# One written sequence of all steps in place of a list scheduler, in a fused attention and Fourier-mixing kernel

## The chip, the cores and the metric

The kernel runs on one core of a Trainium2 chip. A core has a matrix engine (TensorE, PE here), three engines for elementwise work (VectorE, DVE; ScalarE, ACT; GpSimd, POOL), and a queue engine (SyncE, SP) that issues transfers; POOL issues transfers too. Each engine runs its own list of instructions strictly in order, and lists wait for one another through semaphores. The metric is the time of one execution in device microseconds; the median of 3 runs before is 578.95 us (578.54 to 579.04).

## The reference

Inputs are q, k, v (8 batches, 12 heads, 448 tokens, 64 per head) and two weight matrices, 768 x 3072 and 3072 x 768; all float32.

```python
q_n = q / (norm(q) + 1e-6);  k_n = k / (norm(k) + 1e-6)
attn = softmax(q_n @ k_n.T / tau)              # tau = 0.1
x = (attn @ v) as (8, 448, 768)
u = x + real(fft over 448 tokens and 768 channels)(x)
un = (u - mean(u)) / sqrt(var(u) + 1e-6)
out = u + relu(un @ w_ch1) @ w_ch2
```

## The kernel before, in words

Everything of a batch b carries the suffix _b in the names of its steps. A batch goes through three stages.

**Attention.** The loads (ld_q, ld_k, ld_t for the tails on SP, ld_v on POOL) bring in q, k, v. The norms are squares on ACT (sq, L759 and L883), sums on DVE (ss, L762 and L885), then ln, nrm on ACT (L698, L700), eps and rcp on DVE (L701, L702), and the scaling by them (sc, L781 and L785 on DVE or POOL in batches 0 and 1, L896 on POOL later). In batches 0 and 1 the scaled rows are transposed by matmuls (tk, tq, tt, L808 to L833) and copied out of PSUM (ek, eq, et, L799 and L843); from batch 2 on a transposing transfer on SP does it (tr, L902). Then, for each of six pairs of heads j, come the scores (qk j, L973, and L986 for the tail tokens), the exponentials on ACT (ex j, L951), the product with v (pv j, L1004 and L1010), and its division by the sums on DVE (rd j, x j, L1028 and L1030).

**Fourier transform.** Sums and differences of halves on DVE (fa, f0, f1, g, e, L1047 to L1094) shorten it, then there are two groups of matmuls with cosine and sine tables (fs, L1134 and L1138; fd, L1181, L1188, L1191), with a copy between (te, L1159), and the sums that give u (qe on ACT, pq and u on DVE, L1222, L1233, L1245). Each tile of 128 tokens is normalised (ba, L1270; bs, L1275; ln2, rs, L1278 and L1280; un, L1282) and transposed into UNT, in batch 0 by matmuls (tn, L1292, copied out by eu, L1300), later by a transfer on SP (tru, L1303).

**Feed-forward.** h (L1350) multiplies by w_ch1, with a relu on ACT or DVE (L1366) after every 512 columns of PSUM; y and m (L1494) multiply by w_ch2. In the m products two tiles of tokens are done with seven products of half size in place of eight, for which DVE adds up pieces of the hidden values (s1 to s4, L1593); in the last two batches the first multiplication is done so too (p, L1445, with its sums c and k). A result is put together on ACT, POOL and DVE (fa, fm, fv, L1514 and L1519; fin, L1530) and stored (st on SP, sc_ on POOL, L1552).

**What sets the order.** Each step is added to a plan with its engine (or a choice of engines), its duration, a priority, and the steps that it depends on. `schedule` then makes the order of every engine at once: it goes through a modelled time, and at each point picks, among the steps that are ready, the one with the best priority; steps that can run on ACT or DVE go to the one that takes them first. The table SHIFT adds a number to the priority of 338 steps. `emit` writes each engine's list in that order. Before it, `fill` puts filler matmuls (L1737) into PE's list where the plan has PE idle for at least 0.36 us. PSUM is handed out in the plan too: two slots "M" for the feed-forward and three double slots "G" for the rest; a step that needs a slot waits for the last user of the one it gets.

In the plan, a qk that directly follows an h, y, m or p step is charged 0.095 us more (MODE), and a step of DVE that falls into one of certain POOL steps is moved behind its piece (PORT, PIECE).

Of the kernel before, what the change touches and what calls it, by code (L numbers as in the profile page):

```python
# [79 lines left out]
SHIFT = {  # L80
    "iotad": {0: 76.7149}, "tpd": {1: 15.2941}, "ktd0": {0: 169.0303}, "ix3": {0: -59.6164}, "ix4": {0: 735.3976}, "vz1": {0: 116.8365},
    "pads": {0: 761.6515}, "sins": {0: 15.0098}, "ldt0": {0: 217.8585}, "ldt1": {0: -95.8889}, "sind": {0: -207.551}, "sinp": {0: 240.8715},
# [59 lines left out]
}  # L142

# [58 lines left out]
class Plan:  # L202
# [54 lines left out]
    def schedule(self):  # L257
# [46 lines left out]
        for op in self.ops:  # L304
            if cnt[op] == 0:
                put(op)
# [1491 lines left out]
```

## Time and profile before

| | |
|---|---|
| Runs | 578.95 us median (578.54 to 579.04) |
| Span of the profiled execution, first to last instruction | 575.2 us; the page gives no total for this execution, and the median run is 3.75 us above the span |
| Busy: PE, DVE, ACT, POOL | 555.8, 430.6, 385.3, 220.3 us |
| Filler matmuls | 156 |
| First matmul, end of the last | 7.46 us, 571.7 us |
| First h0_0 (start of the feed-forward of batch 0) | 48.46 us |
| Transfers | 62.20 MB, mean 108 GB/s, highest in the first 100 us |

A line of the groups gives the code line, the engine, the operation, output<-input and count, then busy time and the mean of one, then the idle time ahead of it and what ended it. In a line of the timeline the first number is the start in us, the second the time from the first start to the last end of the merged instructions; a wait stands in brackets at the end. A wait is put down to the releaser that came last by the profile.

### The profile page before, as it was taken

Reading aid. Unit: us, or ns where it says so; the run is one execution under the profiler, and the core shown is the slowest. Engines: PE = TensorE matmul, PEld = TensorE weight load, DVE = VectorE, ACT = ScalarE, POOL = GpSimd, SP = SyncE. Lnnn points to the kernel's source line nnn. Section 1 sums busy time; section 2 is a strip of 40 time slices with the busy share of each in tenths; the row PEclk is TensorE's granted clock in tenths of the full one; section 3 lists DMA queues with packets and bytes.
Section 4 is the critical chain, followed back from the end, with each engine's and each line's share of the span. In section 5 each row is a group of like instructions: output and inputs, shape, how many; then the busy total and the mean of one; then the engine's idle time right before and its main releaser. Section 6 shows DMA issues by size and latency. Waiting matters only on the chain.

```text
span 575.2 us, 16313 instructions
## 1 busy us (share of the span) xinstructions
PE 555.8 (97%) x6766; PEld 436.2 (76%) x6766; DVE 430.6 (75%) x917; ACT 385.3 (67%) x724; POOL 220.3 (38%) x332
## 2 busy tenths in 40 slices
PE   3899999999999999999999999999999999989997
PEld 3569787676787686878788787778778787959694
DVE  8989968996669869975669669776778579986262
ACT  7898885564876885687558875577637853747270
POOL 7534414356329544612370724523270210041303
PEclk9999999999999999999999999999999999999999
DMA  9999999975459739952595429743591210023001
GB/s 188 224 233 171 166 186 130 171 152 111 111 94 103 178 76 135 142 127 62 112 121 93 102 80 147 150 84 85 89 113 29 43 57 28 2 43 72 28 28 56
DMA packets 187898, 62.20 MB, mean 108 GB/s; under 512 B 166800, under 2 KB 185616, under 8 KB 187824
## 3 DMA queue, kind: packets, MB, share of 16 engines
q1 hardware_dynamic: 129856, 38.35, 33.7%
q0 software_dynamic: 57968, 22.81, 30.9%
q8 instruction: 53, 0.87, 0.6%
q14 instruction: 21, 0.17, 0.1%
HBM read 51.90 MB, written 11.01 MB: 109 GB/s over the span
## 4 chain that ended last, share of the span: by engine, by line
PE 60%; DVE 4%; ACT 2%; issue 0%; DVEq 0%; ACTq 0%
PE PS L1494 23%; PE PS L1350 20%; PE PS L1445 6%; PE PS L1010 4%; PE PS L973 3%; DVE U L1233 1%; PE PS L1004 1%; PE PS L986 1%; ACT E L951 1%; DVE ACG L1222 1%; ACT F L1275 1%; PE PS L1134 1%; PE PS L1191 1%; DVE SM L885 1%; DVE HQ L1593 1%
## 5 line engine op out<-in xcount | busy, mean ns | idle before, releaser
L1350 PE MATMUL PS<-UNT,W1b 128*128 128x256 bf16 (+1 forms) x1872 | 186.1, 256 | 1.2 <-DMA UNT<-F 0.6
L1350 PEld LDWEIGHTS PS<-UNT,W1b 128*128 128x128 bf16 x1872 | 155.5, 98 | 20.1 <-issue 2.7
L951 ACT ACTIVATE E<-PS 128x900 bf16<-128x900 f32 (+1 forms) x192 | 148.0, 827 | 19.1 <-PE PS L973 16.6
L1494 PE MATMUL PS<-W2b,HQ 128*128 128x384 bf16 x768 | 133.1, 326 | 0.0
L896 POOL TENSOR_TENSOR QH<-STG,SM 128x256 bf16<-128x256 f32 x126 | 82.3, 679 | 91.9 <-DVE SM L702 73.3
L1494 PEld LDWEIGHTS PS<-W2b,HQ 128*128 128x128 bf16 x768 | 73.3, 98 | 46.2 <-issue 0.7
L1519 POOL TENSOR_TENSOR OUTB<-OUTB,U 128x192 f32<-128x192 f32 x66 | 43.2, 675 | 138.5 <-ACT OUTB L1514 137.3
L1366 ACT ACTIVATE HQ<-PS 128x512 bf16<-128x512 f32 x81 | 48.2, 595 | 40.0 <-PE PS L1350 39.5
L1494 PE MATMUL PS<-TX,HQ 128*128 128x384 bf16 (+2 forms) x408 | 69.7, 321 | 1.8 <-ACT MV L1278 1.6
L883 ACT ACTIVATE QH<-STG 128x384 f32<-128x384 f32 x84 | 42.7, 520 | 25.8 <-DVE SM L885 21.3
L1494 PEld LDWEIGHTS PS<-TX,HQ 128*128 128x128 bf16 x408 | 38.4, 98 | 25.7 <-ACT MV L1278 2.0
L1593 DVE TENSOR_TENSOR HQ<-HQ 128x1536 bf16<-128x1536 bf16 (+1 forms) x69 | 49.5, 721 | 9.9 <-ACT HQ L1366 7.1
L885 DVE TENSOR_REDUCE SM<-QH 128x6 f32<-128x384 f32 x84 | 44.7, 544 | 11.3 <-ACT QH L883 11.0
L1010 PE MATMUL PS<-VB,E 128*128 128x65 bf16 x1152 | 51.4, 193 | 0.0
L1366 DVE TENSOR_SCALAR HQ<-PS 128x512 bf16<-128x512 f32 x45 | 31.0, 688 | 23.8 <-PE PS L1350 23.4
L1010 PEld LDWEIGHTS PS<-VB,E 128*128 128x128 bf16 x1152 | 47.7, 97 | 1.2
L1552 POOL DMA_INDIRECT out_dram<-OUTB,IDX x21 | 23.8, 1134 | 56.9 <-DVE OUTB L1530 51.7
L1004 PE MATMUL PS<-VZ,E 128*128 128x130 bf16 x192 | 41.6, 219 | 0.5 <-ACT E L951 0.2
L973 PE MATMUL PS<-QK 64*128 64x225 bf16 (+2 forms) x864 | 39.6, 227 | 0.1
L1233 DVE SCALAR_TENSOR_TENSOR U<-ACG,X 128x768 bf16<-128x768 f32 (+4 forms) x39 | 39.1, 1015 | 0.8
L1530 DVE TENSOR_TENSOR OUTB<-PS,OUTB 128x384 f32<-128x384 f32 x33 | 18.2, 553 | 25.7 <-PE PS L1494 21.9
L1514 ACT ACTIVATE OUTB<-PS 128x384 f32<-128x384 f32 x33 | 16.1, 488 | 29.5 <-PE PS L1494 29.1
(191 smaller groups left out, 793.6 us busy)
## 6 DMA issues: line engine op xcount, KB each, us to landing
STG<-in_q_dram SPq DMA_DIRECT2D x18, 384.0 KB, 4.0
STG<-in_k_dram SPq DMA_DIRECT2D x18, 384.0 KB, 3.8
VB<-in_v_dram POOLq DMA_DIRECT2D x24, 192.0 KB, 7.1
W1b<-in_moe_w_ch_dram POOLq DMA_DIRECT2D x12, 384.0 KB, 7.7
W2b<-in_moe_w_ch_dram POOLq DMA_DIRECT2D x12, 384.0 KB, 7.2
out_dram<-OUTB SPq DMA_DIRECT2D x7, 384.0 KB, 3.4
W2b<-in_q_dram SPq DMA_DIRECT2D x2, 576.0 KB, 10.0
W2b<-in_k_dram SPq DMA_DIRECT2D x2, 576.0 KB, 10.7
```

The lines of the kernel that those rows point to most:

```text
L885: P.add("dve", lambda v, o=SS[:, i, H // ns * x:H // ns * (x + 1)], sq=sq: v.tensor_reduce(o, sq.rearrange("p (h d) -> p h d", d=DH), AX.X ...
L896: r = v.tensor_tensor(v3(qh)[:, h:h + 4], v3(buf)[:, h:h + 4], RN[:, i, h:h + 4].unsqueeze(2).to_broadcast((128, 4, DH)), AluOp.mult)
L951: return a.activation(o, self.PS[:, bk:bk + nc_, 0:SQ2], ACTF.Exp, scale=1.0 / self.tau)
L973: i = pe.matmul(self.PS[:, bk + h, c0:c0 + n], self.KT[r, jj, kt * 128:(kt + 1) * 128], self.QT[r, jj, cols], start=True, stop=True)
L1004: r = pe.matmul(o, st(6), self.VZ[:, j, :], start=not split, stop=(split and i == 0), skip_group_check=True)
L1010: r = pe.matmul(o[:, 65 * h:65 * h + 65], st(2 * kt + h), self.VB[:, kt, 2 * j + h, :], start=(split and i == h == kt == 0), stop=((not sp ...
L1233: self.snu.append(P.add("dve", lambda v: v.scalar_tensor_tensor(two(U[o0:o0 + n, ut, :]), src, 1.0, two(X[i0:i0 + n, x, :]), AluOp.mult, A ...
L1350: r = pe.matmul(self.PS[:, bk, x * n:(x + 1) * n], self.W1b[:, j, ft * 128:(ft + 1) * 128], self.UNT[:, j, cs], start=(j == 0), stop=(j == ...
L1366: return e.activation(o, i, ACTF.Relu) if e is self.nc.scalar else e.tensor_relu(o, i)
L1494: r = pe.matmul(self.PS[:, bk, 0:n], lhs(f), rhs(f), start=(start and f == 0), stop=(stop and f == NF // 2 - 1), skip_group_check=True)
L1519: r = g.tensor_tensor(self.OUTB[:, ob, xs], self.OUTB[:, ob, xs], self.U[:, ut, xs], AluOp.add)
L1593: P.add("dve", lambda v: v.tensor_tensor(cs(o), cs(a), cs(bq), op), 0.16 + 0.3 * len(ks), -0.5, f"{nm}{ks[0]}_{b}", reads=rd, writes=[x fo ...
```

## The change

The table SHIFT and the choice by priorities go. In their place stands SEQ, a list of all 2850 steps in the order in which the plan takes them. An entry is 5 x (number of the step) + (number of the engine: 0 PE, 1 ACT, 2 DVE, 3 POOL, 4 SP), so it fixes both the order on each engine and the engine of each step that has a choice. `schedule` goes through the list and works out times as before (they still decide PSUM slots and where filler goes); it no longer decides on an order. The steps, their dependences and their instructions are the same, but for one: the step finz_7 near the end also counts as a writer of OUT1.

```diff
-SHIFT = {
-    "iotad": {0: 76.7149}, "tpd": {1: 15.2941}, "ktd0": {0: 169.0303}, "ix3": {0: -59.6164}, "ix4": {0: 735.3976}, "vz1": {0: 116.8365},
...
-}
+SEQ = [
...
+    7569, 9719, 8443, 8473, 8453, 8449, 8459, 9799, 9774, 7685, 7690, 7682, 7697, 7216, 7206, 7700, 7970, 7976, 8000, 7705, 7711, 7715, 7720, 7730, 7735,
...
+]
@@ schedule
-        while left:
-            best = None
-            for e in self.ENGS:
-                cands = []
-                for op in ready[e]:
-                    rt = rtime(op, e)
...
-                tmin = min(c[0] for c in cands)
-                t, op = min((c for c in cands if c[0] <= tmin + 1e-9), key=lambda c: (c[1].prio, c[1].seq))
...
-            t, e, op = best
-            for e2 in op.engs:
-                ready[e2].remove(op)
+        for code in SEQ:
+            op, e = self.ops[code // 5], self.ENGS[code % 5]
+            assert all(d.start is not None for d in op.deps.union(op.order))
+            t = max(rtime(op, e), free[e])
+            if op.acquire is not None:
+                t = max(t, slot_time(op)[0] + op.margin)
+            if e == "sp" and sync[-2]:
+                t = max(t, sync[-2].end - DMA_LAT)
             op.eng = e
...
-                                f"finz_{b}", reads=self.unames(b, u1), writes=["OUT1z"], after=(m7,), tiles=(b1,))
+                                f"finz_{b}", reads=self.unames(b, u1), writes=["OUT1z", "OUT1"], after=(m7,), tiles=(b1,))
...
-            op.prio = round(op.prio + SHIFT.get(op.name, {}).get(k, 0), 4)
         self.est = self.P.schedule()
```

Decoded and set beside the order before, engine by engine (steps; steps that leave their former order, as the least number that would have to be moved):

| | PE | ACT | DVE | POOL | SP |
|---|---|---|---|---|---|
| steps before | 969 | 693 | 859 | 195 | 134 |
| steps after | 969 | 672 | 880 | 195 | 134 |
| out of order | 168 | 280 | 370 | 72 | 43 |

109 steps change their engine: 60 from ACT to DVE, 39 from DVE to ACT, 5 from DVE to POOL, 5 from POOL to DVE. The places that the prediction speaks of, before and after (a step that stands several times has several parts):

```text
SP, first loads       before  q1 k0 q0 t0 q2 t1 k1 t2 k2
                      after   q1 t0 t1 k0 q0 k1 q2 t2 k2
POOL, batch 0         before  ld_v2 ld_v0 ld_v1 ld_v3 ktd0 scQ0 ... W1_0
                      after   ld_v2 ktd0 ix6 ld_v1 ld_v3 ix0 scK0 ld_v0 W1_0
ACT, batch 0          before  ex2 ex2 ex2 ex2 et2 et2 ex3 ex3 ex3 ex3
                      after   ex2 ex2 ex2 ex2 ex3 ex3 et2 ex3 ex3           (the other et2 on DVE)
DVE, batch 0          before  u0 u0 u0 ba0 un0 u1 u1 eu00 u1 u1
                      after   u0 u0 ba0 un0 ssT0_1 eu01 cd0 u1 u0          (eu00 on ACT, behind bs0)
PE, second h0_0       before  h19 h20 tn1 tn2 tq0_1 h21 h22 h23 tt0_1 tk0_1 tq2_1 tk2_1 qk00_1 tk1_1 tq1_1 h0 h1
                      after   h19 tq1_1 tt0_1 tq2_1 tq0_1 tn1 tn2 h20 tk0_1 h21 h22 h23 tk1_1 qk00_1 h0 tk2_1 h1
DVE, batch 1          before  pq1 pq1 ba0 u1 u224 fin11_0 u1 ss4_2 ba1 un0 u1 ss4_2 ba3 ba2 fin20_0 un1
                      after   pq1 pq1 u1 u224 ss3_2 u1 ba1 fin11_0 un0 ss3_2 ba2 ktd2 un1
PE, batch 1           before  m20_1 m60_1          after   m20_1 qk00_2 m60_1
DVE, batch 2          before  un0 fin31_1 u1 un1   after   un0 fin31_1 un1 fin21_1 u1
DVE, batch 6          before  pq1_7 pq1_7 s11 c31 u1_7 s12 u224_7 s30 ba0_7 s20
                      after   c31 c31 s10 c2r1 c3r1 s12 s11 ba3_7 s30 s20 pq1_7 pq1_7
PE, batch 4           before  h10_2 h11_2 h20_2 ... h23_2 y02_2 (3) y12_2 (3) y22_2 (2) qk00_4 y22_2
                      after   h10_2 qk00_4 h11_2 h20_2 ... h23_2 qk0t_4 y02_2 (3) qk10_4 y12_2
POOL, batch 4         before  fv0p_2 sc6_4 sc0_5 sc5_4   after   fv0p_2 sc6_4 sc5_4
SP, batch 4           before  tr6_4 ld_k0_5 ld_q1_5 ld_q0_5 tr5_4   after   tr6_4 tr5_4 ld_k0_5
```

More of the change, by code (lines that the diff above doesn't have):

```diff
@@ L78 @@
 }
-SHIFT = {
-    "iotad": {0: 76.7149}, "tpd": {1: 15.2941}, "ktd0": {0: 169.0303}, "ix3": {0: -59.6164}, "ix4": {0: 735.3976}, "vz1": {0: 116.8365},
-    "pads": {0: 761.6515}, "sins": {0: 15.0098}, "ldt0": {0: 217.8585}, "ldt1": {0: -95.8889}, "sind": {0: -207.551}, "sinp": {0: 240.8715},
[59 rows of a table removed]
-}
+SEQ = [
[117 rows of a table added]
+]
 LATE = {r"W[12]_\d+": 1.5, "tmd": 2.0, r"sq\d_\d": 1.5, r"sq[KQT]\d_1": 1.5, r"ktd\d": 2.0, r"qdup\d": 2.0, r"qk\d._[2-7]": 1.5, r"pv\d\d_[2-7]": 1.5, r"pv\d\d_1": 1.0, r"h\d+_[1-7]": 0.5}
@@ L257, in schedule @@
     def schedule(self):
-        nxt = {}
-        cnt = {}
-        for op in self.ops:
-            cnt[op] = len(op.deps.union(op.order))
-            for d in op.deps.union(op.order):
-                nxt.setdefault(d, []).append(op)
-        ready = {e: [] for e in self.ENGS}
         port = []
@@ L298, in drain @@
             return qs
-        def put(op):
-            for e in op.engs:
-                ready[e].append(op)
-        for op in self.ops:
-            if cnt[op] == 0:
-                put(op)
-        left = len(self.ops)
         slots = {n: [None] * k for n, k in self.pools.items()}
@@ L322, in slot_time @@
             return free_at[-1][0], [i for _, i in free_at]
-        while left:
-            best = None
-            for e in self.ENGS:
-                cands = []
-                for op in ready[e]:
-                    rt = rtime(op, e)
-                    if op.acquire is not None:
-                        st = slot_time(op)
-                        if st is None:
-                            continue
-                        rt = max(rt, st[0] + op.margin)
-                    if e == "sp":
-                        rt = max(rt, sync[-2].end - DMA_LAT if sync[-2] else 0.0)
-                    cands.append((max(rt, free[e]), op))
-                if not cands:
-                    continue
-                tmin = min(c[0] for c in cands)
-                t, op = min((c for c in cands if c[0] <= tmin + 1e-9), key=lambda c: (c[1].prio, c[1].seq))
-                if e in ("act", "dve"):
-                    wait = tmin + 0.7 * op.times[e][1]
-                    t2, op2 = min((c for c in cands if c[0] <= wait), key=lambda c: (c[1].prio, c[0]))
-                    if op2.prio >= 9 and (op.prio > op2.prio + 60 or op2.prio < 40 and op.prio > op2.prio + 0.5 and t2 < tmin + 0.25):
-                        t, op = t2, op2
-                if best is None or (t, e) < best[:2]:
-                    best = (t, e, op)
-            t, e, op = best
-            for e2 in op.engs:
-                ready[e2].remove(op)
+        for code in SEQ:
[6 more added lines that the diff above has]
+                t = max(t, sync[-2].end - DMA_LAT)
             op.eng = e
@@ L390, in schedule @@
             self.order[e].append(op)
-            left -= 1
-            for n in nxt.get(op, ()):
-                cnt[n] -= 1
-                if cnt[n] == 0:
-                    put(n)
         return max(op.end for op in self.ops)
@@ L1725, in build @@
             self.ffn(b)
-        seen = {}
-        for op in self.P.ops:
-            k = seen[op.name] = seen.get(op.name, -1) + 1
-            op.prio = round(op.prio + SHIFT.get(op.name, {}).get(k, 0), 4)
         self.est = self.P.schedule()
```

175 rows, old and new, of tables (SEQ, SHIFT) are left out of this document.

## The prediction

> **What bounds the kernel now.** I read the page first, then the time by stretches, then who made TensorE (PE) wait, then the chain of waits and single places of the timeline. From the page, the span and PE's row:
>
> ```profile
> span 575.2 us, 16313 instructions
> PE 555.8 (97%) x6766; PEld 436.2 (76%) x6766; DVE 430.6 (75%) x917; ACT 385.3 (67%) x724; POOL 220.3 (38%) x332
> ```
>
> The same by stretches (length, busy time of PE, PEld, DVE, ACT, POOL, then PE's granted clock):
>
> ```profile
> 0.00:48.40 48.40, 35.94 (x518) 27.82 (x518) 43.20 (x103) 41.44 (x67) 27.32 (x58) 1.00 1.31 211
> 48.40:78.40 30.00, 29.27 (x414) 25.01 (x413) 26.11 (x63) 26.07 (x52) 11.77 (x17) 1.00 1.30 166
> 78.40:118.00 39.60, 38.98 (x379) 27.77 (x380) 31.79 (x75) 25.90 (x56) 14.35 (x22) 1.00 0.98 158
> 118.00:190.00 72.00, 71.88 (x733) 55.14 (x732) 55.47 (x107) 47.83 (x90) 39.05 (x50) 1.00 0.73 118
> 190.00:260.00 70.00, 69.76 (x835) 53.97 (x833) 55.14 (x123) 52.84 (x109) 31.55 (x45) 1.00 0.73 129
> 260.00:504.00 244.00, 243.92 (x3149) 195.19 (x3148) 181.16 (x380) 159.03 (x292) 77.55 (x114) 1.00 0.49 82
> 504.00:506.30 2.30, 0.68 (x5) 0.20 (x3) 1.88 (x4) 1.38 (x4) 1.17 (x1) 1.00 0.02 4
> 506.30:571.70 65.40, 65.38 (x744) 51.12 (x744) 35.54 (x69) 30.78 (x59) 17.23 (x30) 1.00 0.19 44
> 571.70:575.20 3.50, 0.00 (x1) 0.00 (x0) 0.29 (x1) 0.00 (x0) 0.36 (x1) 0.89 0.31 112
> ```
>
> Part of PE's time at the start is filler (line 1737, matmuls that only keep PE at work):
>
> ```profile
> 0.00:48.40 48.40, 12.66 (x150) 9.88 (x150) 1.00 1.31 211
> 48.40:78.40 30.00, 0.59 (x8) 0.35 (x6) 1.00 1.30 166
> ```
>
> And PE's waits from 78.4 on (line, releaser: us, times, longest):
>
> ```profile
> PE PS L1494 <- ACT MV L1278: 1.6, 1, 1.6
> PE PS L1350 <- DMA UNT<-F: 0.6, 1, 0.6
> PE PS L986 <- ACT E L951: 0.2, 1, 0.2
> ```
>
> The reader is to see two regimes. Up to 48.4 us (the first h0_0, the first step of the feed-forward part) PE has 48.4 - 35.9 = 12.5 us of nothing and 12.7 us of filler: there the chain through ScalarE (ACT, 41.4 of 48.4 busy) and VectorE (DVE, 43.2 busy) sets the time. From there to 571.7 PE is full: it stands 0.73 + 0.62 + 0.12 + 0.24 + 0.08 + 1.62 + 0.02 = 3.4 us in 523, and 0.6 more is filler. An order can't shorten the matmuls (the granted clock is 1.00 as long as PE works), so the change can win only at the start and in these 4 us; it can lose anywhere, because each engine works strictly in its list's order, and one late step holds all behind it.
>
> **The change part by part.** It neither adds nor removes a step: 2850 before and after. I decoded the list (number = 5 x step + engine) and set both orders side by side. 109 steps change engine, 60 from ACT to DVE and 39 back, so DVE gets 21 more; out of their former order are 168 of 969 on PE, and many on the others. Since PE has so little slack, I price the places where it stood, in time order.
>
> (a) The start. ACT's idle time in the exponentials of batch 0:
>
> ```profile
> 25.68 0.55 ACT L951 ACTIVATE E<-PS 128x450 bf16<-128x450 f32 x1 [0.27 <-PE PS L986]
> 27.05 0.67 ACT L843 ACTIVATE KTD<-PS 64x192 bf16<-64x192 f32 x2 [0.81 <-PE PS L833]
> 27.99 0.92 ACT L951 ACTIVATE E<-PS 128x900 bf16<-128x900 f32 x1 [0.27 <-PE PS L973]
> ```
>
> The new order puts one copy of 0.67 / 2 = 0.33 us (et2_0) on DVE and the other behind two ex3_0 steps, so up to 0.33 + 0.27 + 0.81 + 0.27 = 1.7 us of ACT's time can go. A second place is the way to h0_0:
>
> ```profile
> 45.84 0.55 DVE L1245 SCALAR_TENSOR_TENSOR U<-PS,X 128x384 bf16<-128x384 f32 x1
> 47.85 0.55 DVE L1300 CAST UNT<-PS 128x384 bf16<-128x384 f32 x1
> 48.46 0.73 PE L1350 MATMUL PS<-UNT,W1b 128*128 128x128 bf16 x10
> ```
>
> Before, a third u0_0 (0.55) stands ahead of ba0_0 and un0_0, and two u1_0 (0.55 each) ahead of the cast eu00_0 that frees h0_0. The new order moves all three behind: 0.5 at the first, and 0.3 to 0.5 at the second, where bs0_0 on ACT is now the last thing ahead of a copy. All of it together is 1.7 + 1.0 = 2.7. Against it stands the new order of the first loads (rival B). I take -1.5, a little over half, because DVE's row of this stretch leaves little room for what it receives; bounds -2.7 and +0.5 (a copy more on a full DVE, 0.55).
>
> (b) 48.4 to 78.4 us: 0.73 idle and 0.59 filler. Before, tn1_0, tn2_0 and seven transposes of batch 1 stand between h20_0 and the second h0_0, five of them behind the last h23_0; now they are spread from h19_0 to the second h1_0, with products between. I take -1.0; bounds 0 and -1.3.
>
> (c) 117 us: PE waits 0.6 for the transposed tile UNT. Between pq1_1 and un1_1 DVE's list loses two ss4_2, a u1_1 and fin20_0 and gains two ss3_2 and a ktd2: the tile leaves earlier. -0.6; bounds 0 and -0.6.
>
> (d) 118 to 260 us: 0.36 idle. qk00_2 now stands ahead of the product m60_1 that waited for s20_1, and un1_2 ahead of a u1_2. -0.3; bounds 0 and -0.4.
>
> (e) 504 us, the largest. PE waits, by the releaser's name for ACT, but in the code for s20_6, the DVE step that writes what m61_6 reads:
>
> ```profile
> 499.96 1.02 DVE L1222 TENSOR_TENSOR ACG<-PS,ACG 128x388 f32<-128x388 f32 x2
> 501.70 0.95 DVE L1233 SCALAR_TENSOR_TENSOR U<-ACG,X 97x768 bf16<-97x768 f32 x1
> 503.40 1.76 POOL L1519 TENSOR_TENSOR OUTB<-OUTB,U 128x192 f32<-128x192 f32 x2 [35.16 <-ACT OUTB L1514]
> 503.48 1.28 DVE L1593 TENSOR_TENSOR HQ<-HQ 128x1536 bf16<-128x1536 bf16 x1
> 505.22 0.96 DVE L1593 TENSOR_TENSOR HQ<-HQ 128x1536 bf16<-128x1536 bf16 x1 [0.39 <-DVE MV L1270]
> 506.32 0.97 PE L1494 MATMUL PS<-TX,HQ 128*128 128x384 bf16 x5 [1.64 <-ACT MV L1278]
> ```
>
> s20_6 ends at 505.22 + 0.96 = 506.18 and PE goes on 0.14 later. Ahead of s30_6 and s20_6 stood two pq1_7 (1.02), u1_7 (0.95) and u224_7; now all of them stand behind. u224_7 pays for two short relus that DVE receives there, the rest is 1.97 us of DVE, more than PE's 1.64. What then comes later is un1_7 and its transpose; another u1_7 that stood ahead of un1_7 goes behind it too, which pays for most. -1.5; bounds 0 and -1.6.
>
> The row shows s20_6 starting at 505.22, just after POOL's two pieces end (503.40 + 1.76 = 505.16), though DVE was idle 0.39. The Trainium skill, SBUF — State Buffer, section "SBUF: two separate sides", says that DVE and GpSimd share one pair of ports as an exclusive lock, and that the loser blocks for the whole instruction. The trace agrees, and it speaks against this place: should s20_6 come just behind the start of POOL's step again, it would wait one piece, 1.76 / 2 = 0.9, and (e) would bring 0.7 in place of 1.5, the sum 0.8 less.
>
> (f) Entering a qk step (its matmuls use 64 rows):
>
> ```profile
> 264.58 1.31 PE PS L1350 x12
> 311.26 1.42 PE PS L1350 x12
> 82.16 0.34 PE L1010 MATMUL PS<-VB,E 128*128 128x65 bf16 x6
> 82.34 1.03 PE L1350 MATMUL PS<-UNT,W1b 128*128 128x256 bf16 x8
> 216.85 0.35 PE L1010 MATMUL PS<-VB,E 128*128 128x65 bf16 x6
> 217.12 0.37 PE L973 MATMUL PS<-QK 64*128 64x225 bf16 x4
> ```
>
> Next to a qk, twelve matmuls take 1.42, elsewhere 1.31. The plan charges this only where a qk follows a product directly: 50 times before, 43 now, 7 x 0.11 = 0.8 to win. But behind a pv step the qk costs the same: from the last six matmuls of a pv to the next step 0.18 to a product, 0.27 to a qk. Counted behind anything but a qk, entries are 95 before and 96 now. So 0; bounds -0.8 and +0.1.
>
> (g) The step finz_7 also writes OUT1 now, so it waits for the store of the tile before. That store lies a whole tile of products earlier; 0. The tail of 3.5 us stays.
>
> (h) New waits of PE, which no row of before can show. Lower bound 0; upper bound: all that (a) to (e) remove, 4.9, since the order of before shows that an order can hold that much. Nearer to the long stretch 260 to 504, where the old order left 0.08 us in 244: +1.0.
>
> Sum: -1.5 - 1.0 - 0.6 - 0.3 - 1.5 + 0 + 1.0 = -3.9, so a span of 571.3. The page gives no total time for its execution; the median of the runs shown, 578.95, lies 3.75 above its span. Kept, that makes 575.0.
>
> **The rivals.** A, the forecast: 575.0.
>
> B, the start brings nothing, as its loads set it. On SP's queue the first k and q loads of batch 0 now stand behind both pairs of tail loads, and on POOL the load ld_v0_0 behind scK0_0. For it: the DMA share of that stretch is 1.31, the highest of all. Against it: the bytes are the same, and the larger k1 load is now ahead of q2, which ACT takes later. Without (a): 575.0 + 1.5 = 576.5.
>
> C, no change: the waits move to other places and (h) reaches its upper bound: 575.0 + 3.9 = 578.9. For it: 109 changes of engine and a plan that gains only by its own durations. Against it: the places (c), (d), (e) are freed by more than their waits.
>
> D, slower: the attention of batch 4 is drawn too far ahead. Before:
>
> ```profile
> 242.32 2.82 SPq L902 DMA_TRANSPOSE QK<-QH  x1
> 250.15 0.78 PE L973 MATMUL PS<-QK 64*128 64x128 bf16 x24
> QK<-QH SPq DMA_TRANSPOSE x42, 3.1
> 312.68 0.65 PE PS L1494 x4
> ```
>
> The last transpose of its k and q (tr5_4) is issued until 245.14 and lands some 3.1 later, at 248.2, 2.0 ahead of qk00_4. In the new order qk00_4 stands ahead of five h steps and eight y02_2 to y22_2 steps, 13 x 0.65 = 8.5 us of PE work earlier, so it is due at 241.7. If it can only start at s, PE has 8.5 us more left than before had at 250.15; the end moves by 8.5 - (250.15 - s), and of the gains only (e) lies behind it, 1.5: together s - 243.15. For s above that it is slower; at 245.7, half way to 248.2, by 2.55: 581.5. Queued behind it on PE are all these h and y steps; ACT's ex0_4 wait with it. For it: SP held tr5_4 for 2.82 us and it landed last of its batch. Against it: sc5_4, which made tr5_4 late, now goes ahead of batch 5's sc0_5 on POOL, and tr5_4 ahead of three loads of batch 5 on SP.
>
> **How the numbers follow.** A 0.50, B 0.17, C 0.14, D 0.15, and 0.04 for nearly all the upper bounds at once (-2.7 - 1.3 - 0.6 - 0.4 - 1.6 = -6.6, 572.3, or 571.6 with (f)). What a measurement can tell from no change is 0.2%, 1.2 us. Faster: A, B nearly whole and the last, 0.70; within: mostly C, 0.13; slower: D and the tail of C, 0.17. The range goes from 571.8, near all bounds at once, to 580.0, short of D's middle; A's own is 572.5 to 577.
>
> **What would show it.** First h0_0 (line 1350's first matmul) near 47 in place of 48.46; the filler at line 1737 down; the waits of 0.6 at 117 and 1.64 at 504 gone; PE's idle time from there to its end near 1.5. B shows as h0_0 still at 48; D as a wait of line 973 for a transpose between 238 and 248; C as new rows in PE's waits. The forecast is wrong if PE's idle time after h0_0 stays at 3.4 or more, or if h0_0 comes later.

## The result: slower, and where the time stands in the profile after

The changed kernel takes 602.9 us (601.2 to 603.8) where the kernel before takes 579.0 (578.5 to 580.2) beside it: a ratio of 1.041, 95% interval 1.039 to 1.043, so 24 us are lost. The prediction had 575.0 and a range up to 580.0. The profile is of the execution of 603.8 us.

The head of the page after. Lines of the kernel after are those of before plus 14 (L1364 is h, L1508 the y and m products, L987 qk, L910 POOL's scaling); in the experiments with a list of their own they are 2 lower (L1362 is h), in pad2_after 2 or 3 higher.

```profile
span 602.0 us, 16232 instructions
PE 563.2 (94%) x6736; PEld 438.9 (73%) x6736; DVE 436.8 (73%) x938; ACT 371.1 (62%) x703; POOL 226.7 (38%) x332
```

PE is busy 7.4 us longer for the same products and fewer fillers, and idle 38.8 us of its span instead of 19.4. To see where, both kernels are cut at the same steps: h0_0 of the batches 0, 1, 2, 4 and 6. Columns: from:to, length, busy time of PE, PEld, DVE, ACT, POOL with their instructions, PE's granted clock, DMA share, GB/s. Before:

```profile
48.40:118.00 69.60, 68.25 (x791) 52.77 (x790) 57.90 (x137) 51.97 (x107) 26.12 (x38) 1.00 1.12 161
118.00:194.90 76.90, 76.63 (x787) 57.91 (x786) 60.30 (x118) 52.37 (x100) 40.58 (x51) 1.00 0.73 120
194.90:333.20 138.30, 138.21 (x1706) 108.48 (x1707) 102.19 (x221) 100.28 (x195) 59.50 (x86) 1.00 0.65 114
333.20:466.70 133.50, 133.42 (x1667) 105.09 (x1665) 94.36 (x200) 86.72 (x158) 46.24 (x68) 1.00 0.55 87
466.70:575.20 108.50, 103.36 (x1306) 84.15 (x1304) 72.62 (x144) 52.49 (x101) 20.59 (x33) 1.00 0.14 38
```

After:

```profile
51.50:123.20 71.70, 67.90 (x783) 52.18 (x784) 55.57 (x140) 48.25 (x95) 22.46 (x31) 1.00 0.94 139
123.20:207.00 83.80, 78.70 (x794) 59.09 (x795) 59.70 (x118) 55.50 (x108) 44.90 (x64) 0.98 0.79 117
207.00:348.00 141.00, 137.34 (x1672) 107.39 (x1670) 102.92 (x222) 92.26 (x178) 55.10 (x77) 1.00 0.63 104
348.00:493.80 145.80, 138.59 (x1695) 107.44 (x1693) 98.52 (x212) 85.81 (x162) 54.30 (x78) 0.98 0.55 91
493.80:602.00 108.20, 103.88 (x1306) 83.97 (x1304) 75.47 (x153) 47.93 (x99) 21.17 (x33) 1.00 0.13 40
```

The stages grow by 3.1 (the start, 48.4 to 51.5), 2.1, 6.9, 2.7 and 12.3 us; the last shrinks by 0.3. The cuts don't part the work quite alike (x1706 and x1667 of PE before, x1672 and x1695 after), so part of the 12.3 belongs to the 2.7. No single place holds the loss. PE's longest waits behind the start, and the one for UNT (line, releaser: us, times, longest):

```profile
PE PS L1152 <- DVE F L1112: 3.9, 2, 2.8
PE PS L1508 <- ACT OUTB L1528: 3.5, 1, 3.5
PE PS L987 <- DMA QK<-QH: 2.9, 1, 2.9
PE PS L1508 <- DVE HQ L1607: 2.4, 2, 2.1
PE PS L1364 <- DMA UNT<-F: 0.6, 1, 0.6
```

The wait for MV of 1.6 us at 504, the prediction's step (e), is gone. The 0.6 for UNT, its step (c), is still there. The others are new, and most of them are put down to a step of DVE. From h0_0 to PE's last product PE now stands 20.8 us (the five stages, 550.5, less 526.4 busy and 3.3 of tail) where it stood 3.4.

The longest, at 143 us, shows how such a wait comes about. Three engines in order of time; the number behind the start is the duration, the bracket the idle time before it:

```profile
136.10 3.71 POOL L910 TENSOR_TENSOR QH<-STG,SM 128x256 bf16<-128x256 f32 x3 [4.76 <-ACT HQ L1380]
141.01 1.27 POOL L1566 DMA_INDIRECT out_dram<-OUTB,IDX  x1 [0.32 <-POOL QK L934]
...
146.28 0.49 ACT L1528 ACTIVATE OUTB<-PS 128x384 f32<-128x384 f32 x1 [5.18 <-DMA out_dram<-OUTB,IDX]
...
142.89 0.56 PE L987 MATMUL PS<-QK 64*128 64x225 bf16 x8
146.92 4.28 PE L1508 MATMUL PS<-TX,HQ 128*128 128x384 bf16 x15 [3.47 <-ACT OUTB L1528]
```

POOL stands 4.76 us ahead of sc5_2, which then takes 3.71 instead of the usual 1.8. Behind it in POOL's list is a store, sc_2_0, whose last addition on DVE ended at 122.75 + 0.50 = 123.25:

```profile
122.75 0.50 DVE L1544 TENSOR_TENSOR OUTB<-PS,U 128x384 f32<-128x384 f32 x1
```

It goes out at 141; ACT can only then overwrite its buffer (fa0_1 at 146.28), and PE's m60_1 needs that copy.

Why does sc5_2 take twice its time? POOL's pieces and DVE's steps seem to hold each other up. More of it between 237 and 245 us:

```profile
237.56 3.05 POOL L910 TENSOR_TENSOR QH<-STG,SM 128x256 bf16<-128x256 f32 x4
242.33 2.64 POOL L1533 TENSOR_TENSOR OUTB<-OUTB,U 128x192 f32<-128x192 f32 x4
...
239.43 1.47 DVE L1068 TENSOR_TENSOR F<-ACG 128x512 bf16<-128x512 bf16 x2
241.53 1.65 DVE L1061 TENSOR_TENSOR ACG<-X 128x512 bf16<-128x512 bf16 x2
```

These DVE steps lie beside pieces of POOL's, and two of them take 1.47 and 1.65 us, where two of the median below would take 0.85. Over the whole run, first min/median/max in ns of one of these steps, and of POOL's scaling piece:

```profile
L1068 DVE TENSOR_TENSOR F<-ACG x48: 406/424/843, 38.4 to 511.0; 128x512 bf16<-128x512 bf16 x48
...
L910 POOL TENSOR_TENSOR QH<-STG,SM x126: 603/612/1387, 107.4 to 462.1; 128x256 bf16<-128x256 f32 x126
```

The largest DVE step is its median and 0.42 more; a whole scaling piece is 0.61.

**What the code says of it.** The old scheduler knew of this: a DVE step that falls into a piece of POOL's is put behind the piece's end. Both versions have the same lines for it:

```python
            if e == "pool" and op.piece:
                port.append((t, op, op.piece))
            elif e == "dve" and op.port and port and port[-1][1].end > t:
                ...
                d += y - t
```

The charge is made only against the last POOL step that has already been taken. The old scheduler took steps in order of their modelled time, so POOL's step had been taken. The new loop takes them in the order of SEQ, and nothing asks SEQ to be in order of time. If POOL's entry stands behind the DVE entry in the list, neither is charged. Counted by the plan's own start times: in the old order 47 DVE steps start inside a POOL step, and for 2 of them POOL's entry comes later; in the new one 67 do, and for 55 POOL's entry comes later. With the charge switched off, the new list's reckoned end doesn't move at all (566.2); with the same order on every engine but the entries taken in order of time it is 592.5, against 572.5 for the old order; 18 of these 26 us are the charge, the rest is what else is reckoned as the list comes, such as the sharing of transfers. These are the code's own sums and no times of the chip. They say that the new list's claim of 6.3 us was a claim of a replay that left something out; what the chip makes of it is for the runs to say.

### The profile page after: what moved, and what is told of

It is laid out like the page before. It is cut to its first block, busy times and chain, and to the rows that moved or that the text cites. A ratio compares the mean times of both kernels' runs of the same rounds, so it can differ in the third digit from the quotient of the medians.

```text
span 602.0 us, 16232 instructions
## 1 busy us (share of the span) xinstructions
PE 563.2 (94%) x6736; PEld 438.9 (73%) x6736; DVE 436.8 (73%) x938; ACT 371.1 (62%) x703; POOL 226.7 (38%) x332
## 5 line engine op out<-in xcount | busy, mean ns | idle before, releaser
L1364 PE MATMUL PS<-UNT,W1b 128*128 128x256 bf16 (+1 forms) x1872 | 188.1, 257 | 3.5 <-DVE OUTB L1544 0.7
L965 ACT ACTIVATE E<-PS 128x900 bf16<-128x900 f32 (+1 forms) x192 | 150.1, 825 | 44.4 <-PE PS L987 35.2
L1364 PEld LDWEIGHTS PS<-UNT,W1b 128*128 128x128 bf16 x1872 | 156.6, 98 | 24.0 <-issue 2.2
L1508 PE MATMUL PS<-W2b,HQ 128*128 128x384 bf16 x768 | 133.6, 327 | 0.0
L910 POOL TENSOR_TENSOR QH<-STG,SM 128x256 bf16<-128x256 f32 x126 | 85.8, 708 | 117.7 <-DVE SM L716 77.6
L1508 PEld LDWEIGHTS PS<-W2b,HQ 128*128 128x128 bf16 x768 | 73.2, 98 | 46.1 <-issue 0.7
L1533 POOL TENSOR_TENSOR OUTB<-OUTB,U 128x192 f32<-128x192 f32 x66 | 45.2, 705 | 125.6 <-ACT OUTB L1528 113.4
L1508 PE MATMUL PS<-TX,HQ 128*128 128x384 bf16 (+2 forms) x408 | 73.4, 332 | 8.3 <-ACT OUTB L1528 3.5
L1380 ACT ACTIVATE HQ<-PS 128x512 bf16<-128x512 f32 x78 | 46.3, 595 | 38.1 <-PE PS L1364 37.9
L1508 PEld LDWEIGHTS PS<-TX,HQ 128*128 128x128 bf16 x408 | 39.0, 101 | 35.8 <-issue 7.1
L1607 DVE TENSOR_TENSOR HQ<-HQ 128x1536 bf16<-128x1536 bf16 (+1 forms) x69 | 52.3, 767 | 2.3 <-ACT HQ L1481 0.9
L1024 PE MATMUL PS<-VB,E 128*128 128x65 bf16 x1152 | 53.2, 193 | 0.0
L1024 PEld LDWEIGHTS PS<-VB,E 128*128 128x128 bf16 x1152 | 48.4, 97 | 1.7
L987 PE MATMUL PS<-QK 64*128 64x225 bf16 (+2 forms) x864 | 40.5, 229 | 4.0 <-DMA QK<-QH 2.9
L1042 DVE RECIPROCAL RD<-PS 128x8 f32<-128x8 f32 (+1 forms) x49 | 9.8, 202 | 38.3 <-PE PS L1024 35.4
L987 PEld LDWEIGHTS PS<-QK 64*128 64x128 bf16 x864 | 25.7, 95 | 16.2 <-issue 9.6
```

The lines of the kernel that those rows point to most:

```text
L910: r = v.tensor_tensor(v3(qh)[:, h:h + 4], v3(buf)[:, h:h + 4], RN[:, i, h:h + 4].unsqueeze(2).to_broadcast((128, 4, DH)), AluOp.mult)
L965: return a.activation(o, self.PS[:, bk:bk + nc_, 0:SQ2], ACTF.Exp, scale=1.0 / self.tau)
L987: i = pe.matmul(self.PS[:, bk + h, c0:c0 + n], self.KT[r, jj, kt * 128:(kt + 1) * 128], self.QT[r, jj, cols], start=True, stop=True)
L1024: r = pe.matmul(o[:, 65 * h:65 * h + 65], st(2 * kt + h), self.VB[:, kt, 2 * j + h, :], start=(split and i == h == kt == 0), stop=((not sp ...
L1364: r = pe.matmul(self.PS[:, bk, x * n:(x + 1) * n], self.W1b[:, j, ft * 128:(ft + 1) * 128], self.UNT[:, j, cs], start=(j == 0), stop=(j == ...
L1380: return e.activation(o, i, ACTF.Relu) if e is self.nc.scalar else e.tensor_relu(o, i)
```

## The experiments

Each kernel is compared with the kernel before, on the same chip. "us more" is the ratio less one, times 579.

| kernel | median us | ratio to before, 95% | us more |
|---|---|---|---|
| the change | 602.9 | 1.041 (1.039 to 1.043) | 23.9 |
| timed_fill | 600.9 | 1.040 (1.038 to 1.042) | 23.0 |
| store_first | 598.2 | 1.034 (1.033 to 1.036) | 19.9 |
| thin_after | 580.9 | 1.0026 (1.0013 to 1.0040) | 1.5 |
| thin_before | 576.8 | 0.9966 (0.9954 to 0.9979) | -2.0 |
| pad2_after | 588.1 | 1.0153 (1.0127 to 1.0178) | 8.9 |
| pad2_before | 580.0 | 1.0017 (1.0004 to 1.0030) | 1.0 |
| front_new | 581.5 | 1.0055 (1.0039 to 1.0072) | 3.2 |
| loads_old | 580.8 | 1.0039 (1.0023 to 1.0054) | 2.3 |
| loads_new | 578.3 | 1.0017 (1.0002 to 1.0032) | 1.0 |
| q2_first | 581.1 | 1.0035 (1.0015 to 1.0054) | 2.0 |
| tail_new | 577.7 | 0.9991 (0.9978 to 1.0005) | -0.5 |
| few_moves | 578.5 | 1.0005 (0.9995 to 1.0015) | 0.3 |
| searched | 582.3 | 1.0066 (1.0047 to 1.0084) | 3.8 |
| searched_rest | 577.1 | 0.9985 (0.9976 to 0.9995) | -0.9 |

### POOL's work thinned out

```diff
 # both kernels, scaling (sc) from batch 2 on
-r = v.tensor_tensor(v3(qh)[:, h:h + 4], v3(buf)[:, h:h + 4], RN..., AluOp.mult)
+r = v.memset(qh.bitcast(F32)[:, 32 * h:32 * h + 128], 0.0501)
 # both kernels, POOL's addition of U to the output
-xs = slice(x, x + 192)
+xs = slice(x, x + 48)
```

> The changed kernel, every order, wait and filler as it is, with most of POOL's vector work left out: each of the three pieces of a scaling step (sc, line 910, from batch 2 on) only fills 128 f32 places with a constant instead of multiplying 256 elements, and each piece of line 1533 adds 48 columns instead of 192. So q and k are constants and the output is not the reference's. Theory 1 (DVE's steps stand behind POOL's pieces, which the list's replay did not charge where a POOL entry stands behind the DVE entry in the list, and PE waits for them): at least 12 us off, 582 to 590, DVE's means back (line 1068 near 460 ns, line 1607 near 715). Rival (the loss is in the start, the loads and the transposes, and DVE's longer steps are hidden): no more than 4 us off, 598 or more.

> The same work left out of the kernel before, with its own order. Theory 1 (that order had placed the steps so that POOL's pieces cost PE next to nothing): 0 to 1.5 us off, 577 to 579. Rival (POOL's pieces cost both orders alike, so that the change only added other losses): as much off as in the changed kernel.

With POOL thinned the changed kernel gets back 22 of its 24 us, more than theory 1 had (at 580.9 it is below 582), and the kernel before 2.0. So 20 us of the loss come with POOL's vector work, and the start, the loads and the transposes, whose order is the same here, hold only what is left. The DVE steps before, in the change, and in the change with POOL thinned (busy us, mean ns of one):

```profile
L1047 DVE TENSOR_TENSOR ACG<-X 128x512 bf16<-128x512 bf16 x48 | 22.4, 498 | 0.7
L1054 DVE TENSOR_TENSOR F<-ACG 128x512 bf16<-128x512 bf16 x48 | 20.5, 464 | 0.6
```

```profile
L1061 DVE TENSOR_TENSOR ACG<-X 128x512 bf16<-128x512 bf16 x48 | 25.6, 560 | 0.5
L1068 DVE TENSOR_TENSOR F<-ACG 128x512 bf16<-128x512 bf16 x48 | 23.0, 504 | 1.0 <-DVE SM L899 0.5
```

```profile
L1061 DVE TENSOR_TENSOR ACG<-X 128x512 bf16<-128x512 bf16 x48 | 20.2, 449 | 0.5
L1068 DVE TENSOR_TENSOR F<-ACG 128x512 bf16<-128x512 bf16 x48 | 19.1, 424 | 1.1 <-DVE SM L899 0.6
```

In the old order, too, these steps are longer than with POOL thinned (423 and 425 ns in thin_before), and all of DVE is busy 11.7 us longer (430.6 and 418.9), in the change 18.6 (436.8 and 418.2). So the old order doesn't keep the two engines apart; it pays only 2.0 us for what it has of it, and PE stands no more than 3.4 us there behind the start.

But thinning takes away two things at once: long pieces, and POOL's length. A thinner POOL also sends its stores and loads earlier.

### POOL's length kept, its long pieces taken away

The first try put register moves of POOL's sequencer ahead of each short piece:

```diff
+spin(v, 8)          # eight g.reg_mov
 r = v.memset(qh.bitcast(F32)[:, 32 * h:32 * h + 128], 0.0501)
```

> The kernel before with POOL's vector work thinned out as in the two thin kernels (constants in place of the scaled q and k, 48 of 192 columns added), but with register moves of POOL's own sequencer ahead of each piece, 8 and 7 of them, so that POOL's steps keep about their length while their pieces are short. Theory 1 (the old order hides both POOL's length and its pieces): 577 to 579. Rival (POOL's length costs the old order): 579 or more. What the register moves take is read from the trace.

The one run of pad_before gave 574.7, but it tells nothing new: the steps stayed at 0.50 us, as in thin_before. The profile has no record of the moves, so where their time went can't be read. The second try uses short pieces of vector work:

```diff
+for y in range(6):
+    v.memset(qh.bitcast(F32)[:, 32 * h + y:32 * h + y + 1], 0.0501)
 r = v.memset(qh.bitcast(F32)[:, 32 * h + 6:32 * h + 128], 0.0501)
 ...
+for y in range(x + 48, x + 52):
+    g.tensor_tensor(self.OUTB[:, ob, y:y + 1], self.OUTB[:, ob, y:y + 1], self.U[:, ut, y:y + 1], AluOp.add)
```

> The changed kernel with POOL's vector work thinned out as in the thin kernels (constants in place of the scaled q and k, 48 of 192 columns added), but with six one-element fills ahead of each piece of a scaling step and four one-column additions in each piece of line 1533, so that POOL's steps keep about their old length while no single piece is long. Theory 1 (what costs is that a step of VectorE waits for the end of one long piece of POOL's): as fast as the thinned kernel or nearly, 579 to 586. Rival (what costs is the length of POOL's steps, which makes its stores, loads and scaling late): 592 to 603.

> The same in the kernel before. Theory 1 (that order hides both POOL's length and its pieces): 576 to 579. Rival (POOL's length costs, in this order too, once the pieces are short): above 579.

The padding came out uneven. The head of pad2_after's page, then its groups:

```profile
PE 558.0 (95%) x6736; PEld 435.6 (74%) x6736; DVE 417.4 (71%) x938; ACT 371.0 (63%) x703; POOL 213.9 (36%) x1352
```

```profile
L1070 DVE TENSOR_TENSOR F<-ACG 128x512 bf16<-128x512 bf16 x48 | 19.0, 421 | 1.6 <-DVE SM L899 0.6 <-DVE X L1046 0.5
L1536 POOL TENSOR_TENSOR OUTB<-OUTB,U 128x1 f32<-128x1 f32 x264 | 58.1, 256 | 126.2 <-ACT OUTB L1530 114.4 <-ACT MV L1296 11.0
L1537 POOL TENSOR_TENSOR OUTB<-OUTB,U 128x48 f32<-128x48 f32 x66 | 19.8, 300 | 0.0
```

POOL is busy 213.9 us in place of 226.7; from its first to its last piece a scaling step is now shorter (1.07 us at the median, 1.76 in the change), an addition longer (2.01, 1.25 in the change). No piece is longer than 0.3 us at the mean, and DVE's L1070, which is L1068 of the change, is back at 421. The time is between the two theories' ranges, so both hold a part. By how much the change exceeds the old order, step by step: 23.9 as it is, 8.9 - 1.0 = 7.9 with short pieces, 1.5 + 2.0 = 3.5 with POOL thinned. So 16.0 go with the long pieces (some of it with the shorter scaling steps), 4.4 with POOL's length, and 3.5 with neither; by the intervals each of these is good to 2 us or so. One thing isn't parted here: a fill reads nothing, where the scaling step reads its rows and norms, so for the scaling pieces "short" and "doesn't read" went together. The kernel before, padded in the same uneven way, is 1.0 slower, as the rival had it: POOL's length costs the old order a little too. The 3.5 are about what the start loses, next.

The Trainium skill, SBUF — State Buffer, section "SBUF: two separate sides", gives this its name: the port pair that VectorE and GpSimd share is an exclusive lock, held for a whole instruction. The maximum of 843 and the means that fall to 421 with short pieces agree; that it is the port, and not another resource which lasts as long as a piece, no run here can tell.

### The start alone

```text
front_new   new order up to 43 us on every engine, old order behind it
loads_new   old order; SP's loads q1 t0 t1 k0 q0 k1 q2 t2 k2 in place of q1 k0 q0 t0 q2 t1 k1 t2 k2
loads_old   as front_new, SP's loads as before
q2_first    as front_new, q2 ahead of k1 on SP
```

> The steps that the new order has up to about 43 us stand in the new order on every engine, all others in the old one; the fillers are the old 26. Theory 1 (the front loses by itself: its transposes, loads and POOL steps come later than the plan has them, and nothing behind takes it up): h0_0 near 51 instead of 48.5, and the end 2 to 3.5 us above the kernel before, about 581.0 to 582.5. Rival (the front's lateness is taken up behind it, or comes from something later in the order): within 0.2%, 577.8 to 580.2. The prediction's own term (a) would have it at 577.5.

> The kernel before, its order as it is, but SP's nine loads of batch 0 in the new order (both pairs of tail loads t0, t1 ahead of k0 and q0, k1 ahead of q2). The kernel's own replay has h0_0 1.0 us later for it. Theory 1 (rival B of the prediction: the first loads set the start, and the chip charges the new order more than the replay): h0_0 near 51 instead of 48.5, the end 581 to 582.5. Rival (the loss of the start is made by the order of POOL, ScalarE and VectorE): the end 578.8 to 580.2.

> The kernel with the new front and the old rest, but SP's nine loads of batch 0 in the old order. The replay has h0_0 1.0 us later for it than with the new loads. Theory 1 (the first loads set the start): back to the kernel before or within 1 us of it, 578.5 to 580. Rival (the order of the other engines makes the loss): 581.5 to 583.5.

> The kernel with the new front and the old rest (581.5), with one move on SP: the load of q2 of batch 0 stands ahead of k1's again. ScalarE's third square step, sqQ2_0, for which it stood still for 2.2 us there with the exponentials behind it, has its data earlier; k1's come later. Theory 1 (this landing, 2.7 us later than the list's plan has it, is what makes the front late): 579 to 580.5. Rival (some other load is as late in the new order of ScalarE's steps): 581 to 583.

The start by itself loses 3.2 us, and nothing behind it takes that up: h0_0 comes at 51.69 in front_new, at 48.46 before. The loads' order alone costs the old kernel 1.0, by an interval from 0.1 to 1.9; the new start with the old loads still loses 2.3, and with q2 alone put back 2.0. So the loads aren't it by themselves. ACT's rows say more. Before:

```profile
11.34 0.84 ACT L759 ACTIVATE W2b<-TX 128x768 f32<-128x768 f32 x1 [0.62 <-DMA TX<-in_k_dram]
12.09 1.15 ACT L759 ACTIVATE HQ<-TX 128x1152 f32<-128x1152 f32 x1
13.14 0.93 ACT L799 ACTIVATE QK<-PS 128x384 bf16<-128x384 f32 x2
...
14.92 2.95 ACT L951 ACTIVATE E<-PS 128x900 bf16<-128x900 f32 x4
```

In the change:

```profile
9.91 0.84 ACT L773 ACTIVATE W2b<-TX 128x768 f32<-128x768 f32 x1
12.94 1.16 ACT L773 ACTIVATE HQ<-TX 128x1152 f32<-128x1152 f32 x1 [2.19 <-DMA TX<-in_q_dram]
14.54 0.55 ACT L813 ACTIVATE QK<-PS 128x449 bf16<-128x449 f32 x1
15.12 0.32 ACT L712 ACTIVATE SM<-SM,MV 128x28 f32<-128x28 f32 x1
15.46 0.23 ACT L714 ACTIVATE SM<-SM 128x28 f32<-128x28 f32 x1
15.60 0.47 ACT L813 ACTIVATE QK<-PS 128x384 bf16<-128x384 f32 x1
...
17.19 0.92 ACT L965 ACTIVATE E<-PS 128x900 bf16<-128x900 f32 x1 [0.37 <-PE PS L987]
```

sqQ2_0 waits 2.19 us for q2, and the copies for the first product stand behind it. But it starts only 0.85 later than before (12.94 and 12.09), and the first exponential 2.27 (17.19 and 14.92). The other 1.4 come behind it: before, the two copies follow at once; in the new order two steps of a norm (15.12 and 15.46) stand ahead of the second. Part of that is the spread between executions: from sqQ2_0's start to the first exponential it is 4.25 here and 2.83 before, but 3.51 and 3.83 in tail_new and few_moves, which have the old start. With q2 ahead of k1 the wait goes to k1, and with the old loads too. ACT's waits up to 50 us, in q2_first (the longest is 2.7; in loads_old it is 2.5, for the same load):

```profile
ACT W2b L771 <- DMA TX<-in_k_dram: 3.1, 2, 2.7
```

Three orders of the loads, and each has a square step on ACT that waits 2 us or more for one. What is common to them is the new order on ACT: it reaches its squares with nothing left to do but wait, and has the norm ahead of the second copy. That is read from the rows; a start with ACT's old order and the rest new was not run, so the cause of the 3.2 us is not shown.

### One store moved, and the fillers

store_first moves one entry of the changed list, sc_2_0, ahead of sc5_2, ix10 and qdup2 on POOL; timed_fill only sorts SEQ by time, which adds 35 fillers.

> The changed kernel with one POOL step moved: the store sc_2_0 stands ahead of sc5_2 and ix10 and qdup2, which it had been behind. Nothing else differs, the fillers included. Theory 1 (the wait of 3.7 us at 143 us, m60_1 for fa0_1 for this store, is lost for good, and the half-pitch products behind it with it): 3 to 5.5 us off the changed kernel, 597.4 to 599.9, and m60_1 at 142 to 143.5. Rival (another chain is as late there, by the kernel's replay taken in order of time, which gives no gain for this move): 601.5 to 604.

> The changed kernel with the order of every engine as it is. Only the list's entries are sorted so that the kernel's own replay takes them in order of time; its ends then come out later, and it sets 56 fillers instead of 21 into the gaps that it sees on PE. Theory 1 (the time is lost in waits on other engines, and the slower clock behind the longest waits is a smaller part): the waits stay, the granted clock goes from 0.991 to 0.995 or more, the time to 597 to 601. Rival 1 (the slower clock is what costs most): below 590. Rival 2 (the fillers don't stand at the waits): 601.5 to 604.

The store alone gives back 24 - 20 = 4 us, in theory 1's range, though the replay in order of time promised nothing. So that replay isn't the chip either. m60_1's own place hardly moved (146.92 to 146.57, where theory 1 had 142 to 143.5): the profile is of the slowest execution, 601.5 us, which had begun later, with its first product at 18.01 in place of 16.59. Its wait there is 2.14 in place of 3.47:

```profile
146.57 0.66 PE L1506 MATMUL PS<-TX,HQ 128*128 128x384 bf16 x3 [2.14 <-DVE HQ L1605]
```

It now waits for a step of DVE. So this store's place in POOL's list costs by itself, beside the pieces. But in thin_after, with the store where the change has it, PE's wait for ACT's copy is gone as well; so these 4 us overlap with the 16 and 4.4 above and don't add to them.

The wait also cost clock. The products of L1508 in the change, in the stretch behind it (length, busy, granted clock):

```profile
146.90:150.40 3.50, 3.48 (x12) 0.51 0.90 224
```

For 3.5 us behind the stand PE had half its clock, from 150.4 to 155.0 us it had 1.00 again, so a wait of 3.5 cost 1.7 more. The Trainium skill, TensorE: Matmul & The Clock Gate, section "Part 1: The HAM clock gate", has the clock halved after an idle window of some 3.4 us and back after as long at work, and these rows agree. At 398 us a shorter stand, 2.88 us, was followed by a lower clock too, which that window doesn't lead one to expect:

```profile
398.10:402.00 3.90, 3.90 (x61) 0.69 0.71 115
```

So was one of 2.12 us: from 375.7 to 379.0 us the clock was 0.50. One of 2.76 us at 246.92 was not (1.00 behind it), so the length of a stand alone doesn't tell. Over the run the mean clock is 0.991, where it is 0.999 before; an estimate from these two is 0.008 x 602 = some 5 us of the 24, and three slow stretches at about 1.7 each come to the same. The fillers of timed_fill bring the clock to 1.0 in two executions (596.7 and 597.1 us) and to 0.997 in the other four (600.8 to 602.3); by the ratio it is only 0.9 us better, so the clock's share isn't settled closer than that. The greater part of the loss is not clock, and the slow stretches follow the waits.

### The tail, and lists that are searched with the replay in order of time

```text
tail_new       old order up to 493 us, new order behind it
few_moves      tail_new; te1_2 one place ahead of nrm3, rs0_7 one ahead of fm1_6 on ACT
searched       a new list from the old one by single moves; replay in order of time, mean of five replays
searched_rest  the same, all steps up to 52 us kept in the old order
```

> The old order up to about 493 us, the new one from there on, with 26 fillers. Theory 1 (the prediction's term (e) holds by itself: s20_6 is no longer behind pq1_7, u1_7 and u224_7, and m61_6 doesn't wait): 0.7 to 1.5 us faster than before, 577.5 to 578.3, and the wait of 1.6 us at 504 us gone. Rival (the wait comes back at another step of that stretch): 578.8 to 579.5.

> The old order up to 493 us and the new one behind it, as in the kernel with the new tail alone, and two more single moves on ScalarE: te1_2 one place ahead of nrm3 at 177 us, rs0_7 one place ahead of fm1_6 at 506 us. They are the only single moves that gain over 0.1 us in a replay in order of time. Theory 1 (a move that takes away one wait, with slack left around it, keeps its gain on the chip): 1 to 2 us faster than before. Rival (gains of some tenths get lost in the chip's own spread of durations): within 0.2% of before.

> A new list, found by moving single steps from the old order as the change did, with two differences: each candidate is replayed in order of time, whatever the order of its entries, and is rated by the mean of five replays, four of them with steps up to some per cent longer and transfers up to twice as long. The replay itself then claims only 3.6 us (the change's list claimed 6.3). Theory 1 (the change lost because of what its replay left out, not because a list is fixed): faster than before, 574.5 to 578.0. Rival (any list fitted to fixed durations gives away what the chip needs as slack): 579 or more.

> A list searched like the one of the kernel searched, with the replay in order of time and the mean of five replays, but all entries up to 52 us kept in the old order. The replay claims 3.0 us. Theory 1 (behind the start, a list whose replay charges VectorE for POOL's pieces loses nothing on the chip; what the searched kernel lost was its start): 575 to 578. Rival 1 (what a search gains in the replay is given back in small waits): 578 to 580. Rival 2 (lists made by a search lose several us wherever they are searched): above 580.

tail_new holds the prediction's best step, (e), alone. The wait of 1.6 at 504 is gone, but the time is the same. DVE and PE behind it:

```profile
512.27 0.48 DVE L1294 TENSOR_SCALAR F<-U,MV 128x768 bf16<-128x768 bf16 x1 [0.56 <-ACT MV L1292]
...
516.67 2.00 PE L1457 MATMUL PS<-UNT,W1b 128*128 128x128 bf16 x33 [1.18 <-DMA UNT<-F]
```

What was moved behind s20_6 makes un0_7 and un1_7 late, and PE waits 1.18 for their transpose. few_moves adds nothing that can be measured.

searched is 3.8 us slower, against theory 1. searched_rest is 0.9 faster, with an interval that just leaves out no change; it is the only list that beats the kernel before, by less than 0.2%. About half of the difference between the two is the start: both profiles have their first qk of batch 0 at 15.6, but h0_0 is 2.2 us apart, at 51.85 in searched and at 49.65 in searched_rest, and the spans are 4.0 apart (580.1 and 576.1). Behind the start the list of searched_rest loses nothing that these profiles show: from h0_0 to the end it takes 526.45, the kernel before 526.74. Its groups:

```profile
L1059 DVE TENSOR_TENSOR ACG<-X 128x512 bf16<-128x512 bf16 x48 | 20.0, 438 | 0.6
L1066 DVE TENSOR_TENSOR F<-ACG 128x512 bf16<-128x512 bf16 x48 | 19.8, 440 | 0.5
```

Its DVE steps are at 438 and 440 ns, and PE has no wait above 0.6 from 51 us on. So a fixed list found by a search need not be slow. Of the change's list two parts are seen to lose: the places behind the start where POOL's pieces hit, which its replay left uncharged, and its start. The two searched lists differ from it in two ways, the replay in order of time and the mean over five replays; no run parts them.

## Why the prediction was wrong

The bound was read rightly: PE is full behind the start, so the change could win some 4 us and lose anywhere. What failed is the size of (h), the new waits: +1.0, with an upper bound of 4.9. Measured, PE stands 20.8 us behind h0_0 in place of 3.4, with some 5 us of slower clock behind these stands, and by the difference of the thinned kernels 20 us go with POOL's vector work. The bound was an argument about orders ("the order of before shows that an order can hold that much"), and it holds only for orders that know what delays a step. The new loop, `for code in SEQ`, stands in the code just ahead of the charge that it goes past; I read the list's places one by one and didn't ask what the list had been rated by.

Step by step:

- (a), -1.5 with an upper end of +0.5: the start lost 3.2. Rival B named the loads, but priced them as no gain, and put aside what row 12.94 shows: that k1 is ahead of q2, "which ACT takes later", stood there as harmless, and ACT waits 2.19 us for just this q2. Nor are the loads all of it: with their old order 2.3 us stay. What stands behind that wait in ACT's new list (rows 15.12 and 15.46) was not priced; which part of the start's order loses the 3.2 stays open.
- (b) and (c), -1.6 together: the stage from h0_0 to batch 1's h0_1 grew by 2.1 instead; PE stands 3.8 us in it where it stood 1.35. (c)'s wait of 0.6 for UNT didn't go.
- (d), -0.3: the place became the worst. qk00_2 went ahead of m60_1, as described, but m60_1 then waited 3.47 us for a copy held up by a store in POOL's queue. In the old list that store stands ahead of sc5_2; that it was moved behind it, I had not priced.
- (e), -1.5: the wait went, as said. Alone it brings -0.5, and the interval holds zero: "what then comes later is un1_7 and its transpose" was right, "which pays for most" was not, as PE stands 1.18 for it.
- (f), 0: no run tests it. (g), 0: from PE's last product to the end of the span there were 3.5 us before, and 602.0 - 596.57 - 2.14 = 3.3 now, as said.
- The lock between DVE and POOL stood in the prediction, at (e), with its row and the rule. I weighed it at the one place where it spoke against a gain of mine, and not over the 67 places of the list where it applies. This came nearest to the cause.
- D, the slower rival: its mechanism came at another batch. qk00_4 didn't wait; qk00_6 did, 2.88 us for its transpose:

```profile
398.10 0.78 PE L987 MATMUL PS<-QK 64*128 64x128 bf16 x24 [2.88 <-DMA QK<-QH]
```

- "The forecast is wrong if PE's idle time stays at 3.4 or more, or if h0_0 comes later": both came (20.8 us, and 51.51), and C's sign, new rows in PE's waits, as well.

## What to carry to other kernels

A list found by a search is only as good as the replay that rated it: before reading its places, check what the replay charges, in which order it goes through the entries, and whether an entry can escape a charge by where it stands in the list. The old scheduler priced the contention, and its order left the busiest engine 0.1 us idle in 244, though DVE's steps were stretched there too; a new order can lose that everywhere at once, in waits that are all short. (That the old order is good because of this charge was not tested by itself.) Take a shared resource away in both versions and compare what each gets back: 22 against 2 us said more here than any single wait.

## What the runs showed of the hardware

- Eight register moves of POOL's sequencer ahead of each piece left its steps at 0.50 us (median of a scaling step, with them and without): no cost shows there.
- One-column additions on POOL are dear: 256 ns at the mean for 128x1 f32, beside 300 for 128x48 in the same kernel (rows of pad2_after); at the median they take 189 and 270, and they overlap: at 144.25 us four in a row take 0.62 us.
- In one execution, stands of PE of 3.47, 2.88 and 2.12 us were followed by stretches of slower clock that cost about 1.7 us each, one of 2.76 us by none.
- The start varies from execution to execution by over 1 us with the same steps in the same order: the first product of batch 0 came at 14.47 us before, 15.48 in tail_new and 15.57 in few_moves. One profile can't judge a start to better than that; the medians can.
